# Mirrored filter rows fetched through copies in DRAM instead of reversed on TensorE, with three small edits at the kernel's opening

## The chip, the cores and the metric

The kernel runs on one core of one Trainium2 chip. The metric is the device time of one execution in microseconds (us). The kernel before takes 127.81 us, the median of 3 runs (127.77 to 128.35).

A core has five engines that run their own instruction lists in order and wait for one another through semaphores: TensorE (PE, with its weight loads listed as PEld), VectorE (DVE), ScalarE (ACT), GpSimd (POOL, unused here beyond four memsets) and SyncE (SP). SP only issues DMA transfers in this kernel. ACT issues a few of them at the start and the last one.

## The reference

```python
x = A_x                                             # [1, 2048, 512] bf16
g = sigmoid((x * gate_w).sum(-1, keepdims=True))
X = rfft2(x.astype(f32), axes=(-2, -1))             # [1, 2048, 257] complex
a = irfft2(X * (w_r + 1j * w_i), s=(2048, 512)).astype(bf16)
h = layernorm(x)                                    # over the 512 columns
u = gelu(einsum("bsd,sf->bdf", h, w1) + b1)         # f: 1792
b = (einsum("bdf,fs->bds", u, w2) + b2).transpose(0, 2, 1)
out = g * a + (1 - g) * b
```

Two branches share x. Branch a is a spectral filter: a two-dimensional real FFT over 2048 rows and 512 columns, a product with a complex filter W of 2048 rows and 257 columns, and the inverse FFT. Branch b is a token mixer: a layernorm, a matrix product that contracts the 2048 rows with `w1`, a GELU, and a product with `w2` back to 2048 rows. A gate per row mixes the two.

## The kernel before, in words

Row s of x is split as s = 512 q + 4 p + r: q from 0 to 3, r from 0 to 3, and p on the 128 partitions. A "row group" below is the 128 rows of one (q, r), 128 x 512 elements.

Branch b has two products. The first (function `m1`, line 705) accumulates over the 16 row groups for each of 14 blocks ft of 128 of the 1792 columns of `w1`. The second (`m2`, line 1011) accumulates over the 14 blocks for each of the 16 output row groups. Together they are the bulk of TensorE's work and need little from the other engines.

Branch a is a chain over the engines:

1. DVE combines the four q of x (lines 535 to 542), TensorE applies DFT tables along the rows (lines 554 to 557), ACT copies the result out of PSUM (line 560), and DVE combines again (line 566).
2. A radix-4 step on DVE for each of two frequency classes lt = 0 and 1 (function `radix4`: part e1 in lines 585 and 586, part e2 in lines 590 and 591, part e3 in lines 597 and 598).
3. A DFT along the columns on TensorE (line 653), once for each lt and each of four e. It reads what part e2 (for even e) or part e3 (for odd e) wrote. ACT copies it out (line 660), DVE combines it (lines 669 to 677).
4. The product with the filter on DVE (lines 820 to 842), then the inverse chain: radix-4 on DVE, line 890 to 898 on TensorE, 904 and 906 on ACT, and so on to line 1030.

The product with the filter works on a pair of mirrored frequencies at once, so each row of W is needed twice: at its own place and, for the mirrored frequency, in reversed order of the partitions. Tile `W` has for both parts of W (comp 0: real, comp 1: imaginary), for each lt and e, a slot 0 (own order) and a slot 1 (mirrored). In the kernel before the mirrored slot is filled in two ways. For lt = 1, four DMAs of 128 rows read the DRAM rows backwards. For lt = 0, the rows are loaded into a staging tile `wt` in natural order, TensorE multiplies them with a reversed identity matrix `flip` (functions `wf`, line 757, and `wfn`, line 767), and ACT copies the result from PSUM into `W` (lines 761 and 770). Function `ld_W` issues 16 DMAs for one comp, each of rows of 257 elements, that is 514 bytes.

`wprep` (lines 777 to 781) halves one row of `W` and forms sums and differences of the two slots at the columns 0 and 256 for two later tiny products. It needs all of `W`, for both comps and both slots.

The order of the work is not written by hand. Each piece is a task (`add`) with an engine, an assumed duration, the tasks that it depends on and a priority. A planner (`Plan.order`) runs a simple list schedule: at each moment it gives each free engine the ready task with the lowest priority number. The resulting order is emitted, and each engine then runs its list strictly in that order. For DMAs the planner assumes one rate for the bytes, one stream for all transfers, and that a DMA can be issued only when the eighth before it has landed. That last rule is real in the program: the transfers take turns on eight semaphores, and each waits, on the issuing engine, until the previous user of its semaphore has landed.

At the opening, `warm` (line 356) runs 10 matmuls over a tile of zeros, `presq` (line 361) takes the square root of a constant on ACT, so that the table of the square root is loaded early, and the row groups (q = 0, r = 0) and (q = 2, r = 0) come in two halves of 64 partitions each, one half on SP's queue and one on ACT's. The layernorm statistics of the first group start with line 487, the root is in line 511, the first normalised group in line 521.

Of the kernel before, what the change touches and what calls it, by code (L numbers as in the profile page):

```python
# [264 lines left out]
def kernel(  # L265
# [23 lines left out]
    pool = ctx.enter_context(tc.tile_pool(name="sb", bufs=1))  # L289
    psum = ctx.enter_context(tc.tile_pool(name="ps", bufs=1, space=bass.MemoryType.PSUM))  # L290
    NES = 2

    def sb(shape, dt, tag, bufs=1):
        return pool.tile(shape, dt, tag=tag, name=tag, bufs=bufs)
# [13 lines left out]
    def alloc_first():  # L308
# [19 lines left out]
        t["wt"] = sb([P, 2, 4, WL], BF16, "wt")  # L328
# [28 lines left out]
    NWARM = 10  # L357
    add("PE", 0.42 * NWARM, warm, reads=["warm", "xs"], writes=["warmed"], prio=-5, alloc=["fa"], free=["fa"])

    def presq():  # L360
        A.activation(t["ombb2"][:, 0:1], t["eps"][:], ActF.Sqrt, bias=t["eps"][:, 0:1], scale=1.0)
    add("ACT", 0.05, presq, reads=["eps"], writes=["omg"], prio=-5)


    Q0 = (0, 2, 1, 3)
    for q in (0, 2):
        for n in range(2):
            hp = slice(n * P // 2, (n + 1) * P // 2)
            ld([("xh", q, n)], lambda hp=hp, q=q: t["x"][hp, q, 0, :], x4[hp, q, 0, :], 65536, -9.5 + 0.1 * q, ("SP", "ACT")[n])
        add("DVE", 0.0, lambda: None, reads=[("xh", q, 0), ("xh", q, 1)], writes=[("x", 0, q)], prio=-9)  # L370
# [62 lines left out]
    def ld_W(comp):  # L433
        v = wsrc[comp].rearrange("(e c k) l -> c e k l", e=4, k=4)
        z = wsrc[comp].rearrange("(v u w) l -> w u v l", v=4, u=2)

        def emit():
            W, u = t["W"][:, comp], t["wt"][:, comp]
            dma(u[64:127, :, 0:257], v[65:128, :, 0, :])
            dma(u[0:64, :, 0:257], v[64:128, :, 2, :])  # L440
            dma(u[127:128, 0:2, 0:257], z[0:1, 1, 2:4, :])
            dma(u[127:128, 3:1:-1, 0:257], z[0:1, 0, 0:4:3, :])
            for e in range(4):
                dma(W[:, 1, e, 1, 0:257], v[:, 3 - e, 3, :].rearrange("(o i) l -> o i l", o=4)[:, ::-1])
            for o in range(4):
                dma(W[32 * o:32 * o + 32, 1, :, 0, 0:257], v[96 - 32 * o:128 - 32 * o, :, 1, :])
            dma(W[1:64, 0, :, 0, 0:257], v[1:64, :, 0, :])
            dma(W[64:128, 0, :, 0, 0:257], v[0:64, :, 2, :])
            dma(W[0:1, 0, :, 0, 0:257].rearrange("w (u v) l -> w u v l", u=2), z[0:1, :, 0:2, :])
            dma(t["wn"][:, comp, 0:257], wsrc[comp][1024:1025, :])  # L450
        return emit

    for comp in range(2):
        add("SP", 12.3, ld_W(comp), writes=[("W", comp), ("wt", comp)], prio=17 + 8 * comp, nbytes=300000, after=[a0])
        if comp == 0:
            load_wb(1)
# [292 lines left out]
    for comp in range(2):  # L749
        for lt in (0,):  # L750
            for a in range(2):
                tag = ("fa", "fb")[a]

                def wf(comp=comp, lt=lt, a=a, tag=tag):
                    pw = t["pw", comp, lt, a] = ps([P, 2, L], F32, tag, 2)
                    for i in range(2):
                        T.matmul(pw[:, i], lhsT=t["flip"][:], rhs=t["wt"][:, comp, 3 - 2 * a - i, 0:L], start=True, stop=True)
                add("PE", mm(256, 256), wf, reads=[("wt", comp), "flip"], writes=[("pw", comp, lt, a)], prio=5, alloc=[tag])

                def wfe(comp=comp, lt=lt, a=a):  # L760
                    A.copy(t["W"][:, comp, lt, 2 * a:2 * a + 2, 1, 0:L], t["pw", comp, lt, a][:])
                add("ACT", act(512), wfe, reads=[("pw", comp, lt, a)], writes=[("W~", comp, lt)], prio=3, free=[tag])

    def wfn():
        pw = t["pwn"] = ps([P, 4, 2], F32, "fa", 2)
        for e in range(4):
            T.matmul(pw[:, e], lhsT=t["flip"][:], rhs=t["wt"][:, :, 3 - e, 256], start=True, stop=True)
    add("PE", mm(*[4] * 4), wfn, reads=[("wt", 0), ("wt", 1), "flip"], writes=["pwn"], prio=5, alloc=["fa"])
    wtk = [("W~", comp, 0) for comp in range(2)]
    add("ACT", 0.3, lambda: A.copy(t["W"][:, :, 0, :, 1, 256], t["pwn"][:].rearrange("p e k -> p k e")),  # L770
        reads=["pwn"], writes=wtk, prio=3, free=["fa"])

# [9 lines left out]
    add("DVE", 0.8, wprep, reads=[], writes=[("W", 0), ("W", 1), "wpm"] + wtk, prio=1)  # L782


    for lt in range(2):
# [37 lines left out]
        for comp in range(2):  # L823
            def mul(lt=lt, comp=comp):
                xs = xph(0).rearrange("p (k c l) -> p k c l", k=8, c=2)
                o = (xph(1) if comp == 0 else t["st"][:]).rearrange("p (k c l) -> p k c l", k=8, c=2)
                w = t["W"][:, comp, lt].rearrange("p e s l -> p (e s) l")[:, :, None, 0:L].to_broadcast([P, 8, 2, L])
                V.tensor_mul(o, xs, w)
            add("DVE", tt(4096), mul, reads=["xs", ("W", comp), ("W~", comp, lt)], writes=[("pp", "st")[comp]], prio=pr)
# [249 lines left out]
```

## Time and profile before

| | before |
|---|---|
| median of 3 runs | 127.81 us (127.77 to 128.35) |
| the profiled execution's own time | 127.68 us |
| its span | 125.9 us |
| PE busy | 120.5 us (96%) |
| DVE busy | 113.8 us (90%) |
| ACT busy | 81.0 us (64%) |
| bytes by DMA | 23.12 MB, mean 184 GB/s |

The span runs from the first to the last instruction of the program; the 1.8 us between it and the execution's own time lie around it. Starts in the profile are counted from the span's start. "SPq" rows are the DMA-issuing instructions of SP: their length is the time that SP's sequencer spends on issuing, not the transfer. A PE row's length includes the pipeline's drain, so that two matmuls in a row overlap: the distance between their starts is the cost, 0.216 us for 512 columns.

### The profile page before, as it was taken

The numbers are of one execution on the slowest core, as the hardware profiler recorded it, in microseconds if no ns is written. First come the engines' busy times: TensorE is split into PE (matmuls) and PEld (weight loads), VectorE is DVE, ScalarE is ACT, GpSimd is POOL, SyncE is SP. The second block draws the span as 40 slices with busy tenths as digits, with TensorE's granted clock in tenths as the row PEclk, the third lists the DMA queues.
The fourth block names the chain that finished last, engine by engine and source line by source line (L and its number), as shares of the span: only waits on it lengthen the run. The fifth ranks groups of instructions, "written<-read, shape, count | busy, mean of one in ns | idle before, by whom it ended". The sixth has DMA issues, their size and how long they took to land.

```text
span 125.9 us, 2138 instructions
## 1 busy us (share of the span) xinstructions
PE 120.5 (96%) x743; PEld 68.8 (55%) x756; DVE 113.8 (90%) x273; ACT 81.0 (64%) x165; POOL 0.2 (0%) x4
## 2 busy tenths in 40 slices
PE   6899999999999999999999999999999999999991
PEld 2344555555655476644445555555577767655590
DVE  2699999999999999999999999999988999999651
ACT  0973689699999999999420004722299999952200
POOL 0000000000000000000000000000000000000000
PEclk9999999999999999999999999999999999999999
DMA  1999999994459946799999900000000000006541
GB/s 57 305 371 358 382 365 358 348 315 86 117 119 288 268 86 162 210 413 411 410 408 407 389 25 0 5 0 0 3 0 0 0 5 0 0 21 229 200 180 44
DMA packets 18219, 23.12 MB, mean 184 GB/s; under 512 B 2190, under 2 KB 15904, under 8 KB 18208
## 3 DMA queue, kind: packets, MB, share of 16 engines
q1 hardware_dynamic: 17616, 22.36, 52.6%
q10 hardware_dynamic: 592, 0.62, 1.6%
q8 instruction: 6, 0.10, 0.3%
q14 instruction: 5, 0.04, 0.1%
HBM read 20.86 MB, written 2.10 MB: 182 GB/s over the span
## 4 chain that ended last, share of the span: by engine, by line
PE 73%; DMA 17%; SPq 7%; issue 1%; DVE 0%
PE acc L1011 32%; PE acc L705 20%; DMA wa<-in_B_w_dram 9%; SPq L306 7%; PE fb L1011 5%; DMA wt<-in_A_w_r_dram 5%; DMA x<-in_A_x_dram 3%; PE fb L653 2%; PE fa L653 2%; PE fa L890 2%; PE fb L890 1%; PE fb L705 1%; PE fa L967 1%; PE fb L967 1%; PE fa L1011 1%
## 5 line engine op out<-in xcount | busy, mean ns | idle before, releaser
L705 PE MATMUL acc<-h,wb 128*128 128x512 bf16 x108 | 25.9, 379 | 0.1
L1011 PE MATMUL acc<-gl,wb 128*128 128x512 bf16 (+1 forms) x94 | 23.9, 371 | 0.2
L1011 PE MATMUL acc<-gl,wa 128*128 128x512 bf16 (+1 forms) x97 | 23.8, 371 | 0.1
L1017 ACT ACTIVATE x<-acc,ombb,omg 128x512 bf16<-128x512 f32 x12 | 9.1, 782 | 21.2 <-PE acc L1011 21.2
L1011 PEld LDWEIGHTS <-wa 128*128 128x128 bf16 x126 | 13.5, 113 | 9.9
L1011 PEld LDWEIGHTS <-wb 128*128 128x128 bf16 x126 | 13.3, 113 | 9.3
L705 PE MATMUL acc<-h,wa 128*128 128x512 bf16 x62 | 17.3, 379 | 0.1
L705 PEld LDWEIGHTS <-wb 128*128 128x128 bf16 x112 | 10.7, 98 | 10.6
L705 PEld LDWEIGHTS <-wa 128*128 128x128 bf16 x112 | 10.3, 98 | 10.7 <-DMA wa<-in_B_w_dram 0.8
L487 DVE BATCH_NORM_STATS2 stats<-x 128x6 f32<-128x512 bf16 x14 | 9.5, 679 | 2.1 <-DMA x<-in_A_x_dram 2.0
L560 ACT CAST xp<-fa 128x512 bf16<-128x512 f32 x16 | 9.1, 581 | 1.8 <-PE fa L557 1.8
L735 ACT ACTIVATE x<-x 128x512 bf16<-128x512 bf16 x16 | 10.2, 691 | 0.0
L721 ACT ACTIVATE gl<-acc,b1f 128x512 bf16<-128x512 f32 x11 | 7.9, 718 | 3.2 <-PE acc L705 3.2
L705 PE MATMUL fb<-h,wa 128*128 128x512 bf16 x31 | 9.5, 379 | 0.1
L527 ACT ACTIVATE h<-x,nmr,rstd 128x512 bf16<-128x512 bf16 x11 | 8.4, 808 | 1.1 <-DMA wb<-in_B_w_dram 0.8
L705 PE MATMUL fa<-h,wa 128*128 128x512 bf16 x16 | 5.9, 378 | 0.7 <-DVE h L521 0.6
L653 PEld LDWEIGHTS <-X 128*128 128x128 bf16 x64 | 4.7, 98 | 2.1
L974 ACT ACTIVATE B<-fb,g 128x512 bf16<-128x512 f32 x8 | 5.7, 713 | 0.0
L974 ACT ACTIVATE B<-fa,g 128x512 bf16<-128x512 f32 x8 | 5.6, 705 | 0.1
L660 ACT CAST X<-fb 128x512 bf16<-128x512 f32 x8 | 5.1, 634 | 0.0
L660 ACT CAST X<-fa 128x512 bf16<-128x512 f32 x8 | 5.0, 620 | 0.0
L356 PE MATMUL fa<-xp 128*128 128x512 bf16 x10 | 3.8, 549 | 1.2 <-DVE xp L317 1.2
(169 smaller groups left out, 232.7 us busy)
## 6 DMA issues: line engine op xcount, KB each, us to landing
wb<-in_B_w_dram SPq DMA_DIRECT2D x11, 512.0 KB
wa<-in_B_w_dram SPq DMA_DIRECT2D x7, 512.0 KB
wa<-in_B_w_dram SPq DMA_DIRECT2D x2, 896.0 KB
wb<-in_B_w_dram SPq DMA_DIRECT2D x4, 384.0 KB
out_dram<-x SPq DMA_DIRECT2D x3, 512.0 KB
x<-in_A_x_dram SPq DMA_DIRECT2D x2, 512.0 KB
wa<-in_B_w_dram SPq DMA_DIRECT2D x2, 448.0 KB
rot<-dft_ti SPq DMA_DIRECT2D x1, 768.0 KB
```

What stands on the lines that cost most here:

```text
L306: (eng or nc.sync).dma_start(out=out_ap, in_=in_ap)
L487: V.bn_stats(out=t["stats"][:, j, :], in_=t["x"][:, j // 4, j % 4, :])
L527: add("ACT", 0.71, lambda j=j: A.activation(t["h"][:, j // 4, j % 4, :], t["x"][:, j // 4, j % 4, :], ActF.Identity, bias=t["nmr"][:, j:j ...
L560: add("ACT", act(512), lambda r=r, dq=dq: A.copy(xe(r)[:, :, :, dq, :], t["pa", r, dq][:]), reads=[("pa", r, dq)], writes=[("X", r, dq)], ...
L653: T.matmul(pb[:, k % 2, k // 2], lhsT=t["X"][:, lt, EX[e], c, k, :], rhs=tbl(k, c), start=True, stop=True)
L660: A.copy(t["X"][:, lt, EX[e]].rearrange("p c j l -> p (c j l)").rearrange("p (h c g b) -> p h c g b", h=2, c=2, b=2)[:, :, c], t["pb", lt, ...
L705: T.matmul(t["u", ft][:], lhsT=w[:, j // 4, j % 4, c * P:(c + 1) * P], rhs=t["h"][:, j // 4, j % 4, :], start=(j == jorder[0]), stop=(j == ...
L721: gelus.append(add("ACT", act(512, 1) , lambda ft=ft: A.activation(t["gl"][:, ft, :], t["u", ft][:], ActF.Gelu_apprx_tanh, bias=t["b1f"][: ...
L735: A.activation(t["x"][:, q, r, :], t["x"][:, q, r, :], ActF.Copy, accum_out=t["glog"][:, 4 * q + r:4 * q + r + 1])
L974: A.activation(eo_v(p)[:, n], t["i3", j][:], ActF.Copy, scale=t["g"][:, j:j + 1])
L1011: T.matmul(t["y", j, m][:, cs], lhsT=w[:, o, 512 * q + r:512 * q + 512:4], rhs=t["gl"][:, ft, cs], start=(ft == 0), stop=(ft == NFT - 1))
L1017: A.activation(tbuf(j).rearrange("p h d -> p (h d)"), t["y", j, 0][:], ActF.Identity, bias=t["ombb2"][:, j:j + 1], scale=t["omg"][:, j:j + 1])
```

## The change

- The mirrored slot of both lt is loaded, and nothing is reversed on TensorE. `wf`, `wfn`, their copies on ACT and the staging tile `wt` go.
- For each comp two new DRAM scratch tensors: `fe` (4 x 128 rows) and `fo` (16 x 32 rows). `ld_flip` issues, for each comp, two DMAs from DRAM to DRAM that write rows of W in reversed order into `fe` (the rows for lt = 0) and `fo` (those for lt = 1).
- `ld_nat` issues the loads in natural order, 10 DMAs for each comp, among them the two single-row pieces of the mirrored slot.
- `ld_mir` issues three loads for each comp from `fo` and `fe` into the mirrored slots.
- In the emitted order of SP the four copies come first, where the first load of `wt` was, then the natural loads of comp 0, the four loads of `wb` (the last three blocks of `w1`), the natural loads of comp 1, and the six mirrored loads. The loads of the tables `ti` and `tg` now stand ahead of four loads of `w2`.
- The two first row groups come as one DMA each, q = 0 on SP's queue and q = 2 on ACT's.
- `presq` goes, and `NWARM` is 9 instead of 10.
- All orders follow from the planner. On DVE, `wprep` moves: it stood behind the last combination of line 677, and now stands in the radix-4 step of lt = 1 between part e1 (lines 585 and 586) and part e2 (lines 590 and 591). On TensorE five more matmuls of line 705 come before the first of line 653 for lt = 1: 53 instead of 48 counted from the first that reads `wb`.

```diff
-        t["wt"] = sb([P, 2, 4, WL], BF16, "wt")
...
-    NWARM = 10
+    NWARM = 9
...
-    def presq():
-        A.activation(t["ombb2"][:, 0:1], t["eps"][:], ActF.Sqrt, bias=t["eps"][:, 0:1], scale=1.0)
-    add("ACT", 0.05, presq, reads=["eps"], writes=["omg"], prio=-5)
...
     for q in (0, 2):
-        for n in range(2):
-            hp = slice(n * P // 2, (n + 1) * P // 2)
-            ld([("xh", q, n)], lambda hp=hp, q=q: t["x"][hp, q, 0, :], x4[hp, q, 0, :], 65536, -9.5 + 0.1 * q, ("SP", "ACT")[n])
-        add("DVE", 0.0, lambda: None, reads=[("xh", q, 0), ("xh", q, 1)], writes=[("x", 0, q)], prio=-9)
+        ld([("x", 0, q)], lambda q=q: t["x"][:, q, 0, :], x4[:, q, 0, :], 131072, -9.5 + 0.1 * q, "ACT" if q else "SP")
...
-    def ld_W(comp):
+    def ld_flip(comp):
+        ev = wsrc[comp].rearrange("(e m w) l -> w e m l", e=4, w=2)[0, :, P:2 * P, :]
+        od = wsrc[comp].rearrange("(g i k) l -> k g i l", i=32, k=4)[3]
+
+        def emit():
+            fe = t["fe", comp] = dram.tile([4, P, 257], BF16, tag=f"fe{comp}", name=f"fe{comp}")
+            fo = t["fo", comp] = dram.tile([16, 32, 257], BF16, tag=f"fo{comp}", name=f"fo{comp}")
+            dma(fe[:], ev[:, ::-1])
+            dma(fo[:], od[:, ::-1])
+        return emit
+
+    def ld_nat(comp):
...
-            dma(u[64:127, :, 0:257], v[65:128, :, 0, :])
-            dma(u[0:64, :, 0:257], v[64:128, :, 2, :])
-            dma(u[127:128, 0:2, 0:257], z[0:1, 1, 2:4, :])
-            dma(u[127:128, 3:1:-1, 0:257], z[0:1, 0, 0:4:3, :])
-            for e in range(4):
-                dma(W[:, 1, e, 1, 0:257], v[:, 3 - e, 3, :].rearrange("(o i) l -> o i l", o=4)[:, ::-1])
...
+            dma(W[0:1, 0, 0:2, 1, 0:257], z[0:1, 0, 0:4:3, :])
+            dma(W[0:1, 0, 3:1:-1, 1, 0:257], z[0:1, 1, 2:4, :])
...
+    def ld_mir(comp):
+        def emit():
+            W, fe, fo = t["W"][:, comp], t["fe", comp], t["fo", comp]
+            m = fe[:].rearrange("e (p two) l -> two p e l", two=2)
+            dma(W[:, 1, ::-1, 1, 0:257], fo[:].rearrange("(e o) i l -> (o i) e l", e=4))
+            dma(W[1:64, 0, ::-1, 1, 0:257], m[1, 0:63])
+            dma(W[64:128, 0, ::-1, 1, 0:257], m[0, 0:64])
+        return emit
+
+    FL = (16, 16.1)
     for comp in range(2):
-        add("SP", 12.3, ld_W(comp), writes=[("W", comp), ("wt", comp)], prio=17 + 8 * comp, nbytes=300000, after=[a0])
+        add("SP", 1.1, ld_flip(comp), writes=[("flp", comp)], prio=FL[comp], nbytes=700000, after=[a0])
+    for comp in range(2):
+        add("SP", 5.5, ld_nat(comp), writes=[("W", comp)], prio=17 + 8 * comp, nbytes=300000, after=[a0])
+        add("SP", 1.6, ld_mir(comp), reads=[("flp", comp)], writes=[("W~", comp)], prio=26 + comp, nbytes=500000)
         if comp == 0:
             load_wb(1)
...
-    add("DVE", 0.8, wprep, reads=[], writes=[("W", 0), ("W", 1), "wpm"] + wtk, prio=1)
+    add("DVE", 0.8, wprep, reads=[], writes=[("W", 0), ("W", 1), ("W~", 0), ("W~", 1), "wpm"], prio=1)
```

The functions `wf` and `wfn` with their tasks are deleted from the program.

## The prediction

> **What bounds the kernel now.** I read the page's busy shares first, then the chain, then the waits, and then the timelines of SP, DVE and PE around the place where the filter is loaded.
>
> ```profile
> span 125.9 us, 2138 instructions
> PE 120.5 (96%) x743; PEld 68.8 (55%) x756; DVE 113.8 (90%) x273; ACT 81.0 (64%) x165; POOL 0.2 (0%) x4
> ...
> PE 73%; DMA 17%; SPq 7%; issue 1%; DVE 0%
> ```
>
> PE has work for 96% of the span, and the chain lies on it for 73%; its links through DMA and SP are from the loading phase. PE never waits long after the opening, so it is the bound: matmuls taken away are worth their full length, and every us in which PE has to wait later is added in full. DVE is close behind, in a chain that PE reads from.
>
> The loading of the filter, on SP:
>
> ```profile
> 24.90 2.56 SPq L306 DMA_DIRECT2D wt<-in_A_w_r_dram  x4
> 27.95 7.55 SPq L306 DMA_DIRECT2D W<-in_A_w_r_dram  x11
> 35.55 0.42 SPq L306 DMA_DIRECT2D wn<-in_A_w_r_dram  x1
> 36.01 2.62 SPq L306 DMA_DIRECT2D wb<-in_B_w_dram  x4
> 38.68 2.54 SPq L306 DMA_DIRECT2D wt<-in_A_w_i_dram  x4
> 41.27 8.55 SPq L306 DMA_DIRECT2D W<-in_A_w_i_dram  x11
> 49.87 0.42 SPq L306 DMA_DIRECT2D wn<-in_A_w_i_dram  x1
> ```
>
> (Columns: start, length, instruction.) SP issues without rest from 24.9 to 50.3 us: one DMA takes it 0.35 to 0.69 us. And it waits: of its waits between 24 and 51 us the first is
>
> ```profile
> SPq L306 <- DMA wb<-in_B_w_dram: 4.4, 4, 1.5
> ```
>
> 4.4 us in 4 waits, each for the eighth DMA before. So a slow transfer holds up everything that SP issues from the eighth place behind it.
>
> DVE, where `wprep` stood and where it will stand:
>
> ```profile
> 44.82 1.22 DVE L586 TENSOR_TENSOR st<-X 128x2048 bf16<-128x2048 bf16 x1
> 46.07 0.69 DVE L590 TENSOR_TENSOR X<-xp 128x1024 bf16<-128x1024 bf16 x1
> 46.68 0.68 DVE L591 TENSOR_TENSOR X<-xp 128x1024 bf16<-128x1024 bf16 x1
> ...
> 57.46 0.41 DVE L777 TENSOR_SCALAR W<-W 1x1028 bf16<-1x1028 bf16 x1
> 57.91 0.19 DVE L780 TENSOR_TENSOR wpm<-W 128x16 f32<-128x16 bf16 x1
> 58.21 0.19 DVE L781 TENSOR_TENSOR wpm<-W 128x16 f32<-128x16 bf16 x1
> ```
>
> At 57.5 us all of `W` has been there for long and `wprep` waits for nothing. Its new place is between lines 586 and 590, at 46.1 us.
>
> **The change part by part.**
>
> *Matmuls removed.* Eight of line 757 and four of line 767:
>
> ```profile
> 53.02 0.38 PE L757 MATMUL fa<-wt,flip 128*128 128x256 bf16 x2
> 53.24 0.38 PE L757 MATMUL fb<-wt,flip 128*128 128x256 bf16 x2
> 53.46 0.38 PE L705 MATMUL acc<-h,wb 128*128 128x512 bf16 x1
> 53.67 0.24 PE L767 MATMUL fa<-wt,flip 128*128 128x2 bf16 x4
> 53.78 0.81 PE L705 MATMUL acc<-h,wb 128*128 128x512 bf16 x3
> ```
>
> By the starts, two of line 757 cost 0.22 us and the four of line 767 some 0.2 us at most: 8 x 0.108 + 0.2 = 1.07 us off PE. The five copies on ACT also go; ACT is 64% busy, so that is worth nothing by itself.
>
> *The opening.* The first real matmul (5.56 us) waits for the first normalised group, which hangs on x's first group (statistics start at 3.48) and on ACT's root at 4.58. The halves landed at 2.95 and 3.35 us by their semaphores; one whole load has twice the rows on one queue and shares the transfer engines with the other group: 0 to 0.5 us later. Against it, `presq` (0.30 us at 4.38) no longer stands before the root, and the table load, which waits for nothing, starts earlier, since ACT issues one DMA fewer (0.6 us). The tenth matmul over zeros ended at 4.98, before 5.56, so it was hidden. Between -0.3 and +0.5; I take 0.
>
> *SP's new order and the wait that `wprep` gets.* This decides. `wprep` now needs the last of the six mirrored loads. I follow SP from 24.90, where the first copy is issued.
>
> (a) Which transfer engines carry the copies? The nearest rows are the four 128-row loads from 27.95 on: their DRAM side has an outer dimension of 4, as the `fe` copies have, and each raised its semaphore once early and then four times (30.94, 30.96, 31.48, 31.50 for the first), so four engines carried it, 32 rows each. The last rises of the next three are at 32.77, 34.15 and 35.25: 1.2 us for 32 rows, 37 ns a row; the packets of 514 bytes themselves took 28 ns in the median. I take 34 ns. An `fe` copy then puts 128 rows on each of these four engines, and an `fo` copy (outer dimension 16) 32 rows on every engine: 2 x (128 + 32) = 320 rows in line on four engines, 10.9 us. They start when `b2h`, ahead of them, is through (rises from 28.15 on, take 28.7): the last copy lands at 39.6.
>
> The Trainium skill (DMA: Bandwidth & Descriptors, "Why a DMA increments its semaphore by 16 and not by 1", on how many engines) says that a DMA is spread over the largest number up to 16 that divides the outer dimension of both sides. It would put `fe` on 4 engines and `fo` on 16. The four rises agree; no row of this trace is a copy from DRAM to DRAM.
>
> (b) The first single-row piece of comp 0 is eight places behind the last copy, so it goes at 39.6. With two more issues (0.63, 0.63, 0.42 and 0.05 between) 41.4; the four of `wb` take 2.62, the last starts at 43.4 and SP is free at 44.1.
>
> (c) The same piece of comp 1 is eight behind the last `wb`. That one was issued at 38.01 before and landed between 43.7 (14 engines) and 45.56 (the last two), 5.7 to 7.5 us: here 49.1 to 50.9, take 50.0. The seven issues between need only 3.7 us.
>
> (d) Three issues (1.83) to 51.8, then the six mirrored loads: by the forms of 512, 252 and 256 rows 0.63, 0.54 and 0.63, so the last starts at 55.0. A load of that form was issued at 48.48 and landed at 51.67: 3.2 us. The mirror is complete at 58.2.
>
> (e) DVE stands at `wprep` from 46.1 to 58.2, then does line 781 (0.2) and lines 590 and 591 (1.29 from 46.07 to their end): 59.8. On PE the matmuls of line 653 for lt = 1 wait for that. PE gets there at: 35.63 (first with `wb`) + 42 x 0.216 + 16 x 0.055 + 0.65 + (16 x 0.055 + 3 x 0.216) + 5 x 0.216 = 48.85. Behind it in PE's list stand all 51 matmuls of line 705 that are left and the whole second product: they could run, and cannot pass. PE waits 59.9 - 48.85 = 11.05 us.
>
> What would cover this? ACT and DVE do nothing that PE could use; PE's fillers are behind the waiting instruction. The loads of `w2` start some 5 us later (55.7 instead of 50.4), but their reader (64.5) is moved by 11 us, so they stay hidden.
>
> *After the wait.* Does PE come back at full pace? The opening shows it from rest: weight loads at 1.62, 2.04, 2.47, 2.90, 3.32, 3.75 and 4.18, so 0.43 us for a 512-column matmul, against 0.216 later. After the pause of 0.57 us before 5.56 the pace was 0.216. So between 0 and 7 x 0.21 = 1.5 us; a pause of 11 us is nearer the first, I take 1.5.
>
> The Trainium skill (TensorE: Matmul & The Clock Gate, "Part 1: The HAM clock gate") says that PE falls to half its clock after an idle window of about 3.4 us and needs about as long at work to come back. By it the sum is the one below; without a fall it would be 137.7. The opening agrees; no long pause within the kernel is in this trace.
>
> *Sum,* against the profiled execution's 127.68 (0.13 below the median of the runs): 127.68 - 1.07 + 0 + 11.05 + 1.5 = 139.2 us.
>
> **Rivals.**
>
> 1. *The copies are spread over 16 engines.* Then 128 rows stand on each, they are done by 33.1 and hold up nothing; `wb` starts at 35.3, the single-row piece of comp 1 goes at 43.9 behind the last `wb`, the last mirror is issued at 48.9 and lands at 52.1. PE waits 5.0 us: 131.6, and 130.6 if the last `wb` lands with the early engines. For it: `fe`'s DRAM target is one run of 512 rows. Against: the four rises above.
>
> 2. *Writing rows to DRAM is dearer.* A tenth of the 514-byte packets took 53 ns and more; at 53 ns the 320 rows take 17.0 us, 6.1 more: 145.3. For it: the trace has no such write; against: the packets of stores are not slower than those of loads.
>
> 3. *The mirror is there in time.* It decides in (e): with the last mirror landed by 47.3 us PE does not wait, and the time is 126.6; at 48.4 the matmuls saved are used up; every us later is a us more. If SP never had to wait, its issues would run 24.9 + 4 x 0.67 + 5.6 + 2.7 + 5.6 + 3.2 = 44.7 to the last and land at 47.9: 127.3, no change; with transfers that land a little faster, faster. For it: the issues alone nearly fit. Against: SP waited 4.4 us here already, for `wb` alone, and now has more bytes ahead.
>
> **How the numbers follow.** The forecast (last mirror at 56 to 60 us): 0.65. Rival 1: 0.13. Rival 2: 0.12. Rival 3: 0.10, half of it faster, half the same. About 0.5% (0.6 us) can be told from no change. Faster 0.05, same 0.05, slower 0.90. The range takes in rival 1 and most of rival 2: 130.5 to 145; the forecast's own is 136.5 to 141.5.
>
> **What would show it.** DVE: one idle time of some 12 us before line 781 (or 780), ended by a DMA into `W`. PE: an idle time of some 11 us before line 653, near 49 us, ended by DVE; then weight loads 0.43 us apart for some 3 us. SP: a gap of some 3.5 us that ends near 38.5 us, when the second `fe` copy lands, before the natural load of single rows that stands eight places behind it. No line 757 or 767 on PE. The forecast is wrong if DVE passes `wprep` without idle time, or if the copies raise their semaphores 16 times each within 2 us.

## The result, and the profile after

The changed kernel takes 143.29 us, the median of 6 runs (142.63 to 144.81); the kernel before took 127.79 us beside it (127.68 to 128.35). The ratio is 1.121, with a 95% interval of 1.115 to 1.127. The prediction was 139.2 us, with a range from 130.5 to 145. The profiled execution took 142.63 us. In the experiments below some profiled executions are longer than others of the same kernel; the ratios leave the longer ones out, and where a row is read from such an execution its time stands beside it.

Lines of the changed kernel are 12 higher than before up to the removed functions and 12 lower behind them: line 653 is now 665, 705 is 717, 590 is 602, 777 to 781 are 765 to 769, and 1011 is 999.

From the page of the changed kernel: the span, the busy times, and the chain by engine.

```profile
span 140.8 us, 2108 instructions
PE 122.7 (87%) x743; PEld 68.9 (49%) x743; DVE 113.5 (81%) x273; ACT 79.5 (56%) x159; POOL 0.2 (0%) x4
...
PE 53%; DMA 27%; SPq 15%; issue 1%; DVE 1%; ACTq 1%; DVEq 0%
```

PE was at work for 96% of the span and is at 87%. The chain now lies on DMA and SP for 42% where it was 24%: in the middle of the kernel, PE follows the loads.

SP's timeline of the changed kernel over the filter's loads (start, length, instruction):

```profile
24.50 0.75 SPq L307 DMA_DIRECT2D fe<-in_A_w_r_dram  x1
25.30 3.76 SPq L307 DMA_DIRECT2D fo<-in_A_w_r_dram  x1
29.10 0.85 SPq L307 DMA_DIRECT2D fe<-in_A_w_i_dram  x1
30.00 4.32 SPq L307 DMA_DIRECT2D fo<-in_A_w_i_dram  x1
34.36 7.48 SPq L307 DMA_DIRECT2D W<-in_A_w_r_dram  x9
...
42.34 2.62 SPq L307 DMA_DIRECT2D wb<-in_B_w_dram  x4
45.00 6.80 SPq L307 DMA_DIRECT2D W<-in_A_w_i_dram  x9
...
52.30 0.66 SPq L307 DMA_DIRECT2D W<-fo  x1
...
55.27 1.42 SPq L307 DMA_DIRECT2D W<-fe  x2
56.79 4.32 SPq L307 DMA_DIRECT2D wa<-in_B_w_dram  x7
```

The first natural load is issued at 34.36. In the kernel before, SP's first load of the filter went at 24.90 and its last at 49.87. Two single instructions, the issues of `fo`, hold SP for 3.76 and 4.32 us. Behind them SP waits another 1.7 us, until 39.81, for the landing of the second `fe` copy, whose semaphore the seventh natural load takes.

DVE's timeline of the changed kernel at `wprep`; the brackets give the idle time ahead and what ended it:

```profile
44.95 1.22 DVE L598 TENSOR_TENSOR st<-X 128x2048 bf16<-128x2048 bf16 x1
53.41 0.42 DVE L765 TENSOR_SCALAR W<-W 1x1028 bf16<-1x1028 bf16 x1 [7.24 <-DMA W<-in_A_w_i_dram]
58.69 0.18 DVE L768 TENSOR_TENSOR wpm<-W 128x16 f32<-128x16 bf16 x1 [4.86 <-DMA W<-fo]
61.77 0.19 DVE L769 TENSOR_TENSOR wpm<-W 128x16 f32<-128x16 bf16 x1 [2.90 <-DMA wa<-in_B_w_dram]
61.87 0.69 DVE L602 TENSOR_TENSOR X<-xp 128x1024 bf16<-128x1024 bf16 x1
```

`wprep` waits three times, 15.0 us together: for the natural loads of comp 1, the mirror of comp 0 and the mirror of comp 1. (The last wait is put down to a load of `w2` that landed at about the same moment; the last semaphore rise of the sixth mirrored load is at 61.65.) Line 602, which PE needs, follows.

PE's timeline at the same place:

```profile
47.68 1.24 PE L717 MATMUL acc<-h,wb 128*128 128x512 bf16 x5
62.62 0.61 PE L665 MATMUL fa<-tb,X 128*128 128x128 bf16 x4 [13.70 <-DVE X L602]
63.02 0.63 PE L717 MATMUL acc<-h,wb 128*128 128x512 bf16 x1
63.44 0.63 PE L665 MATMUL fb<-tb,X 128*128 128x128 bf16 x4
...
67.26 0.39 PE L665 MATMUL fa<-tb,X 128*128 128x128 bf16 x4
```

PE stands for 13.70 us, and afterwards a matmul of 512 columns costs 0.43 us (63.02 to 63.44) where it cost 0.216. That lasts 4.64 us for work that takes 2.62 us at the usual pace. The sum closes: 127.68 - 1.07 + 13.70 + 2.0 = 142.3, against 142.63.

### The profile page after: what moved, and what is told of

It reads as the page before. It is cut to its first block, busy times and chain, and to the rows that moved or that the text cites. A ratio compares the mean times of both kernels' runs of the same rounds, so it can differ in the third digit from the quotient of the medians.

```text
span 140.8 us, 2108 instructions
## 1 busy us (share of the span) xinstructions
PE 122.7 (87%) x743; PEld 68.9 (49%) x743; DVE 113.5 (81%) x273; ACT 79.5 (56%) x159; POOL 0.2 (0%) x4
## 4 chain that ended last, share of the span: by engine, by line
PE 53%; DMA 27%; SPq 15%; issue 1%; DVE 1%; ACTq 1%; DVEq 0%
PE acc L999 29%; SPq L307 15%; DMA wa<-in_B_w_dram 11%; PE acc L717 10%; DMA fe<-in_A_w_i_dram 8%; PE fb L999 5%; DMA wb<-in_B_w_dram 4%; DMA W<-fe 4%; PE fa L878 1%; PE fb L878 1%; PE fa L665 1%; PE fb L665 1%; PE fb L955 1%; PE fa L955 1%; ACTq L307 1%
## 5 line engine op out<-in xcount | busy, mean ns | idle before, releaser
L717 PE MATMUL acc<-h,wb 128*128 128x512 bf16 x112 | 27.3, 392 | 0.0
L1005 ACT ACTIVATE x<-acc,ombb,omg 128x512 bf16<-128x512 f32 x12 | 9.7, 824 | 19.9 <-PE acc L999 19.9
L665 PE MATMUL fa<-tb,X 128*128 128x128 bf16 x32 | 3.6, 242 | 13.7 <-DVE X L602 13.7
L717 PE MATMUL fb<-h,wa 128*128 128x512 bf16 x32 | 10.0, 379 | 0.0
L962 ACT ACTIVATE B<-fb,g 128x512 bf16<-128x512 f32 x8 | 7.0, 874 | 0.0
L962 ACT ACTIVATE B<-fa,g 128x512 bf16<-128x512 f32 x8 | 7.0, 870 | 0.0
```

The lines of the kernel that those rows point to most:

```text
L665: T.matmul(pb[:, k % 2, k // 2], lhsT=t["X"][:, lt, EX[e], c, k, :], rhs=tbl(k, c), start=True, stop=True)
L717: T.matmul(t["u", ft][:], lhsT=w[:, j // 4, j % 4, c * P:(c + 1) * P], rhs=t["h"][:, j // 4, j % 4, :], start=(j == jorder[0]), stop=(j == ...
L962: A.activation(eo_v(p)[:, n], t["i3", j][:], ActF.Copy, scale=t["g"][:, j:j + 1])
L1005: A.activation(tbuf(j).rearrange("p h d -> p (h d)"), t["y", j, 0][:], ActF.Identity, bias=t["ombb2"][:, j:j + 1], scale=t["omg"][:, j:j + 1])
```

## The experiments

The first four share 17 runs of the kernel before (127.87 us), the next four share 7 (127.69), the last four share 13 (127.81).

### The opening alone

The kernel before with the three small edits only:

```diff
-        for n in range(2):
-            hp = slice(n * P // 2, (n + 1) * P // 2)
-            ld([("xh", q, n)], lambda hp=hp, q=q: t["x"][hp, q, 0, :], x4[hp, q, 0, :], 65536, -9.5 + 0.1 * q, ("SP", "ACT")[n])
-        add("DVE", 0.0, lambda: None, reads=[("xh", q, 0), ("xh", q, 1)], writes=[("x", 0, q)], prio=-9)
+        ld([("x", 0, q)], lambda q=q: t["x"][:, q, 0, :], x4[:, q, 0, :], 131072, -9.5 + 0.1 * q, "ACT" if q else "SP")
...
-    add("ACT", 0.05, presq, reads=["eps"], writes=["omg"], prio=-5)
...
-    NWARM = 10
+    NWARM = 9
```

> The kernel before with the three edits at the opening alone (whole loads of the two row groups on two queues, no early root, nine zero products). Theory: they are worth next to nothing, the first real matmul starts 0.1 us earlier as in the changed kernel (5.45 against 5.56 us): 127.6 us, between 127.3 and 128.0. Rival: part of the 15 us comes from the opening, by a later first group or a different order: over 129 us.

Measured: 127.75 us (127.43 to 129.24, 12 runs), ratio 0.9999 with the interval 0.9975 to 1.0023. The opening is worth nothing, as the prediction took it. All of the change in time belongs to the filter's rows.

### `wprep` behind the last combination again

The changed kernel with `wprep` pinned where it stood before:

```diff
-    add("DVE", 0.8, wprep, reads=[], writes=[("W", 0), ("W", 1), ("W~", 0), ("W~", 1), "wpm"], prio=1)
+    add("DVE", 0.8, wprep, reads=[], writes=[("W", 0), ("W", 1), ("W~", 0), ("W~", 1), "wpm"], prio=1, after=[pl.last_w["B", 1, 3]])
```

> The changed kernel with the copies as they are, but wprep ordered behind the last combination on DVE, where it stood before. Theory: the cost is the wait of wprep at its early place; the mirror still lands near 61.7 us, DVE gets to wprep near 57.7 us and waits some 4 us, of which PE, which reads DVE's results next near 88 us, pays about 3: 130 us, between 128.5 and 131.5, and no slow matmuls near 62 us. Rival: the copies cost by themselves (their traffic delays other loads): 138 us or more.

Measured: 145.16 us (143.66 to 145.83), ratio 1.131 with the interval 1.125 to 1.136. The expectation fell: the wait of 13.7 us is gone from line 665, and the time is no shorter. The groups of waits of this kernel (the profiled execution took 145.83) show where it went; the columns are the us waited in total, how often, and the longest:

```profile
...
PEld L999 <- DMA wa<-in_B_w_dram: 9.5, 7, 2.0
PE acc L999 <- DMA wa<-in_B_w_dram: 6.5, 7, 1.5
...
DVE wpm L768 <- DMA W<-fo: 5.2, 1, 5.2
```

PE comes to the second product in time and finds no `w2`. On SP the seven loads of `w2` into `wa` were issued at 62.21 (before: 50.40), behind the copies, the natural loads and the mirror. PE takes each as it lands:

```profile
59.67 6.21 PE L717 MATMUL acc<-h,wb 128*128 128x512 bf16 x28
67.35 0.41 PE L999 MATMUL acc<-gl,wa 128*128 128x512 bf16 x1 [1.48 <-DMA wa<-in_B_w_dram]
68.62 0.41 PE L999 MATMUL acc<-gl,wa 128*128 128x512 bf16 x1 [0.86 <-DMA wa<-in_B_w_dram]
69.90 0.61 PE L999 MATMUL acc<-gl,wa 128*128 128x512 bf16 x1 [0.87 <-DMA wa<-in_B_w_dram]
```

One matmul for every 1.27 us, the time in which 512 KB land. So the place of `wprep` decides only which reader of SP's late loads waits. The prediction took the `w2` loads as hidden because "their reader (64.5) is moved by 11 us"; this run is the case in which the reader is not moved by a wait.

### `fe` on sixteen engines

The changed kernel, with the `fe` copies written with an outer dimension of 16 like `fo` (as many rows of the same size, but other rows than the mirrored table needs):

```diff
-            dma(fe[:], ev[:, ::-1])
+            dma(fe[:].rearrange("e (o i) l -> (e o) i l", o=4), wsrc[comp].rearrange("(g i k) l -> k g i l", i=32, k=4)[0][:, ::-1])
```

> The changed kernel with the two fe copies reading as many rows with an outer dimension of 16 instead of 4, so that 16 engines carry them. It copies other rows into the scratch, so the mirrored filter of lt = 0 is not the reference's; amounts and order of all work are the same. Theory: SP was held up by copies on four engines; now they end near 34 us, SP issues the last mirrored load near 49 to 50 us instead of 56.1, it lands near 54.5 instead of 61.7, and PE's wait shrinks from 13.7 to about 7: 136 us, between 134 and 138. Rival: rows written to DRAM are dear on whatever engine: 141 us or more.

Measured: 143.8 us (141.65 to 144.38), ratio 1.114 with the interval 1.107 to 1.121. The expectation fell. SP's timeline of this kernel:

```profile
28.09 1.20 SPq L307 DMA_DIRECT2D fo<-in_A_w_i_dram  x1
29.33 11.91 SPq L307 DMA_DIRECT2D W<-in_A_w_r_dram  x9
41.30 0.41 SPq L307 DMA_DIRECT2D wn<-in_A_w_r_dram  x1
```

The copies are issued without the long holds (1.20 us for the last), but the natural loads take 11.91 us instead, and SP is done with them at nearly the same moment, 41.71 against 42.30. By their semaphores the four copies land at 39.98; in the changed kernel they land at 40.43. The engines that carry `fe` raise its semaphore 16 times here; in the changed kernel it rose once early and four times late (32.16 to 33.78 for comp 0). So `fe` was on four engines, as the prediction's step (a) had it, and it made no difference: 2048 rows of 514 bytes, from DRAM to DRAM, are through at 40 us with 320 of them in line on four engines or with 128 in line on each of sixteen. The stretch from 29 to 34 us shows how, first in the changed kernel, then in this one. The columns are the length, the busy time of PE, PEld, DVE, ACT and POOL, PE's clock, the DMA share and GB/s:

```profile
29.00:34.00 5.00, 5.00 (x37) 3.01 (x36) 5.00 (x9) 4.99 (x9) 0.00 (x0) 1.00 0.47 102
29.00:34.00 5.00, 5.00 (x36) 2.99 (x34) 5.00 (x9) 4.82 (x10) 0.00 (x0) 1.00 1.24 112
```

The DMA share is the packets' time as a share of sixteen engines' time. It is 0.47 where four engines have a long line and the others a short one, and 1.24 here. But the rows move hardly faster: a packet of 514 bytes took 62 ns here in the median of that stretch, where it took 28 ns in the changed kernel. So more engines shortened the line and lengthened the row. What slows the rows on sixteen engines is not shown by any run.

### The copies from GpSimd's queue

The copies are issued by GpSimd from 22.9 us on, and `wprep` is pinned late as in the second experiment:

```diff
-            dma(fe[:], ev[:, ::-1])
-            dma(fo[:], od[:, ::-1])
+            if comp == 0:
+                t["pw"] = sb([1, 8], BF16, "pw")
+                nc.gpsimd.tensor_copy(t["pw"][:], t["gw"][0:1, 0:8])
+            dma(fe[:], ev[:, ::-1], nc.gpsimd)
+            dma(fo[:], od[:, ::-1], nc.gpsimd)
...
-        add("SP", 1.1, ld_flip(comp), writes=[("flp", comp)], ...)
+        add("POOL", 1.1, ld_flip(comp), reads=["gw"], writes=[("flp", comp)], ...)
...
+    add("DVE", 0.8, wprep, ..., prio=1, after=[pl.last_w["B", 1, 3]])
```

> The changed kernel with the four copies issued from GpSimd's queue behind a tiny copy of a piece of gw (landed near 21 us), and wprep at its late place. Theory: SP is not held up, the mirror is complete by about 50 us, wprep waits for nothing at 57.5 us, and the removed matmuls are what is left: 126.6 us, between 126.2 and 127.2, faster than the kernel before. Rival: the copies' share of the four engines delays the last blocks of w1 or the loads of w2 and PE waits elsewhere: 128.5 us or more.

Measured: 144.08 us (141.13 to 145.38), ratio 1.122 with the interval 1.116 to 1.128. The expectation fell again. SP's timeline (the profiled execution took 141.13):

```profile
24.36 17.14 SPq L307 DMA_DIRECT2D W<-in_A_w_r_dram  x9
...
56.69 3.65 SPq L307 DMA_DIRECT2D wa<-in_B_w_dram  x6
```

SP is no longer held by the copies' issue, and its first nine natural loads take 17 us all the same: one of them, of 256 rows, holds it for 4.13 us at its issue, and it waits 5.3 us for `b2h`, the load ahead of them, which was issued at 23.89 and landed at 40.23. The first natural load was issued at 24.36 and landed at 40.86. Another queue does not take the copies off the path of SP's loads. The Trainium skill (DMA: Bandwidth & Descriptors, "Queues, rings and completion order") says that each transfer engine takes turns, packet by packet, between the queues that have work for it; the trace agrees, in which packets of both queues start in every microsecond from 27 to 39 us, while that load needs 16.5 us. `w2` follows at 56.69, 6 us late, and PE waits for it as in the second experiment.

### Without the copies

The copies are left out, the mirrored loads stay where they are and read the weights as they lie:

```diff
-            fe = t["fe", comp] = dram.tile(...)
-            fo = t["fo", comp] = dram.tile(...)
-            dma(fe[:], ev[:, ::-1])
-            dma(fo[:], od[:, ::-1])
+            t["fe", comp], t["fo", comp] = ev, od
```

> The four DRAM copies are left out; the six mirrored loads keep their place and their sizes and read rows of the weights as they lie, so the mirrored half of the filter table holds the wrong rows. Order on PE, DVE and ACT as in the changed kernel. Theory (the copies' own time on the DMA path is what comes late): SP starts on the natural loads at 24.5 in place of 34.36, all behind them is 9.9 us earlier, PE's wait in front of line 665 falls from 13.7 to about 3.8 and the clock stays up: 142.6 - 9.9 - 2.0 = 130.7, between 129 and 133. Rival (the mirrored loads in their new place behind w1's last blocks are late by themselves): the wait stays over 10 us and the time over 138.

Measured: ratio 1.0425 with the interval 1.035 to 1.050, that is 5.4 us over the kernel before. The four executions lie apart, at 132.93, 133.84, 137.34 and 138.29; the ratio is that of the first two, and the profiled one is that of 137.34. By the ratio the copies are worth 10.1 of the 15.5 us (1.121 against 1.0425); by the other two executions it would be 5 to 6 us. The theory was right in sign, but 5.4 us are left that it did not foresee in full. In the profiled execution PE's wait has shrunk but not gone:

```profile
PE fa L662 <- DVE X L599: 7.4, 1, 7.4
DVE wpm L765 <- DMA W<-in_A_w_r_dram: 5.5, 1, 5.5
DVE wpm L766 <- DMA wa<-in_B_w_dram: 3.4, 1, 3.4
```

`wprep` still waits 8.9 us for the mirrored loads, which are issued from 45.36 to 49.84 behind 20 natural loads and four of `wb`, and land until 55.1. So the new order on SP has a price of its own, even with no copies.

### Without the copies, `wprep` late

The edits of the second and the fifth experiment together:

```diff
-            dma(fe[:], ev[:, ::-1])
-            dma(fo[:], od[:, ::-1])
+            t["fe", comp], t["fo", comp] = ev, od
...
+    add("DVE", 0.8, wprep, ..., prio=1, after=[pl.last_w["B", 1, 3]])
```

> As the run without copies, and the line of wprep pinned behind the last step of the first product's DVE work, as in the second experiment (wrong mirrored rows again). Theory: nothing is late any more, w2's loads are issued at about 46 (before: 50.40), and what is left is the saving of the nine matmuls: 126.6, between 126 and 127.8. Rival (the pinned place costs by itself, by which the second experiment could be explained): w2 in time and still over 133.

Measured: 134.26 us (133.65 to 135.74), ratio 1.048 with the interval 1.042 to 1.053. The theory's 126.6 fell, and so did its rival as it was put: `w2` is not in time. Its `wa` loads are issued at 50.53, as before, but the first lands at 56.95 in place of 54.09, since the mirrored loads ahead land until 55.97. And SP's timeline goes on (the profiled execution took 135.74):

```profile
50.53 4.82 SPq L307 DMA_DIRECT2D wa<-in_B_w_dram  x7
55.99 0.33 SPq L307 DMA_DIRECT2D rot<-dft_ti  x1
56.97 0.32 SPq L307 DMA_DIRECT2D tg<-dft_tg  x1
58.30 9.06 SPq L307 DMA_DIRECT2D wb<-in_B_w_dram  x7
```

In the kernel before the first loads into `wb` were issued at 54.19, ahead of `ti` and `tg`. PE stands for them at the second product (4.7 us in three waits, the longest 3.2). Apart from the later landing, two differences could be behind this: that order on SP, or PE's own order, which takes the blocks of `w2` one after the other here. The runs with `w2` first and with `ti` first, below, bear on them.

### Half the copies, `wprep` late

Only `fe` stays; the mirrored rows of lt = 1 are loaded directly, as in the kernel before:

```diff
-            dma(fo[:], od[:, ::-1])
...
+            for e in range(4):
+                dma(W[:, 1, e, 1, 0:257], v[:, 3 - e, 3, :].rearrange("(o i) l -> o i l", o=4)[:, ::-1])
...
-            dma(W[:, 1, ::-1, 1, 0:257], fo[:].rearrange("(e o) i l -> (o i) e l", e=4))
```

> Only the copies fe stay; the reversed half of odd rows is loaded straight from the weights with the four loads for each component that the kernel before has; wprep pinned late. Theory (dose): half the copied rows, so half of their 15.9 us; w2's loads are issued at about 50 to 54 in place of 62.2, up to 4 us later than before: 127 to 133. Rival (a fixed price as soon as anything is copied through DRAM, by waiting for its completion): as the second experiment, over 140.

Measured: 142.48 us (141.32 to 143.31), ratio 1.112 with the interval 1.103 to 1.120. Half the copied rows saved little, against the theory's dose. By the semaphores the two `fe` copies land at 38.29, only 2.1 us earlier than all four: 256 rows stand in line on four engines, where there were 320. That is 33 ns for each of the 64 rows fewer, and the DMA share from 31 to 35 us is 0.26, about four engines of sixteen: here the line on four engines binds. Then 28 natural loads instead of 20 have to go, and `w2` is issued at 60.17. A copy of half the rows on the same four engines gains little.

### The copies into SBUF

As the run without copies, but 2048 rows are loaded into a scrap tile in SBUF at the copies' place:

```diff
+            if comp == 0:
+                t["se"] = sb([P, 2, 4, 257], BF16, "se")
+            dma(t["se"][:, 0], ev.rearrange("e m l -> m e l"))
+            dma(t["se"][:, 1], od.rearrange("(e o) i l -> (o i) e l", e=4))
```

> The same 2048 rows of 514 bytes are copied at the same place of SP's queue, but into a scrap tile in SBUF and not reversed; the mirrored loads read the weights as they lie, as in the run without copies (wrong mirrored rows). Theory (writing rows to DRAM is what is dear): 128 rows on each of 16 engines at the 34 ns of the loads of before = 4.4 us in place of 15.9; SP's natural loads start about 28 to 30, PE's wait is 6 to 8 us: 133 to 137. Rival (a row costs the same wherever it goes, the number of rows is what counts): as the changed kernel, 141 to 144.

Measured: ratio 1.084 with the interval 1.075 to 1.093, or 10.7 us over the kernel before. That lies about midway between the run without copies (5.4) and the changed kernel (15.5), between theory and rival. But it is not the price of the rows alone. The scrap tile is one for both components, so the loads of comp 1 wait until those of comp 0 have landed, a wait that the copies into DRAM do not have. SP's waits from 24 to 40 us (the profiled execution took 152.51):

```profile
SPq L307 <- DMA se<-in_A_w_r_dram: 4.4, 2, 4.1
```

What can be compared is the first half. By the semaphores the 1024 rows of comp 0 land at 31.62 in SBUF, and at 35.91 in DRAM (the run with `fe` on sixteen engines), both issued between 23.7 and 25.5 us behind the same loads. This speaks for rows into DRAM being slower; how much of the copies' cost that makes was not measured.

### Without the copies, `wprep` late, `w2` ahead of `ti` and `tg`

The kernel of the sixth experiment, with the loads of `ti` and `tg` bound to the end of the matmuls that free the first buffer of `wb`:

```diff
-    load("tg", [P, 642], BF16, tabs["tg"], 164352, prio=39.5)
...
-    add("SP", 0.2, ld_ti, writes=["ti"], prio=39, nbytes=754176, after=[...])
+    m4 = [m1t[order.index((NF + 3, jorder[-1]))]]
+    add("SP", 0.2, ld_ti, writes=["ti"], prio=39, nbytes=754176, after=m4 + [...])
+    load("tg", [P, 642], BF16, tabs["tg"], 164352, prio=39.5).deps.update(m4)
```

> As the sixth experiment (no copies, wrong mirrored rows, wprep pinned late), and the loads of ti and tg put back behind the four loads of w2 that the kernel before issues ahead of them. Theory (what was left there is the second product starving for w2: its loads into wb were issued at 58.30 behind ti and tg, in the kernel before at 54.19 ahead of them): the wb loads are issued at about 55.4, PE waits at most 2 us for them, and the time is 126.6 to 129. Rival (the wait comes from the amount of data ahead of the second product, whatever the order, as the whole of w2 starts at 50.5 in both): 132 or more.

Measured: 131.30, 133.65, 133.92 and 133.94 us. The order on SP is that of the kernel before (the `wb` loads are issued at 53.93), and the time is still 3.5 to 6 us over it: 131.30 lies between theory and rival, the other three in the rival's range. PE's timeline of the execution of 133.94:

```profile
63.34 1.67 PE L997 MATMUL acc<-gl,wa 128*128 128x512 bf16 x7
65.54 0.41 PE L997 MATMUL acc<-gl,wb 128*128 128x512 bf16 x1 [0.53 <-DMA wb<-in_B_w_dram]
66.83 0.41 PE L997 MATMUL acc<-gl,wb 128*128 128x512 bf16 x1 [0.88 <-DMA wb<-in_B_w_dram]
68.10 0.49 PE L997 MATMUL acc<-gl,wb 128*128 128x512 bf16 x1 [0.87 <-DMA wb<-in_B_w_dram]
69.36 0.62 PE L997 MATMUL acc<-gl,wb 128*128 128x512 bf16 x1 [0.77 <-DMA wb<-in_B_w_dram]
69.78 3.19 PE L997 MATMUL acc<-gl,wa 128*128 128x512 bf16 x7
```

PE reads seven blocks of `wa` and then, one by one, four of `wb`. The kernel before does the same work in another order (its PE timeline):

```profile
64.35 2.11 PE L1011 MATMUL acc<-gl,wa 128*128 128x512 bf16 x9
66.30 0.38 PE L1011 MATMUL acc<-gl,wb 128*128 128x512 bf16 x1
66.51 1.24 PE L1011 MATMUL acc<-gl,wa 128*128 128x512 bf16 x5
67.59 0.81 PE L1011 MATMUL acc<-gl,wb 128*128 128x512 bf16 x3
```

It already works on the next row groups with the blocks that are there, needs `wb` later and at a slower rate, and never waits. So PE's order of the second product is another thing that moved with the plan.

### The kernel before with `ti` and `tg` first

```diff
-    load("tg", [P, 642], BF16, tabs["tg"], 164352, prio=39.5)
+    load("tg", [P, 642], BF16, tabs["tg"], 164352, prio=34.3)
...
-    add("SP", 0.2, ld_ti, writes=["ti"], prio=39, ...)
+    add("SP", 0.2, ld_ti, writes=["ti"], prio=34.2, ...)
```

> The kernel before with one thing changed: ti and tg are loaded ahead of all seven wb loads of w2, as in the changed kernel. Theory: the four wb loads are issued at about 57 to 58 in place of 54.19 and land some 3 us later; the second product, which reads the first of them at 66.30, waits for them some 2 to 4 us: 129 to 132. Rival (before has slack enough): 127.8, no change.

Measured: 127.71 us (127.69 to 128.32, 10 runs), ratio 0.9986 with the interval 0.9964 to 1.0007. The rival's number held: `ti` and `tg` ahead of `w2`'s `wb` loads cost nothing, although the first of those loads went out at 55.95 and landed at 67.20, later than in the run before this one (65.49). But the planner moved PE's order along with the edit:

```profile
64.37 4.48 PE L1011 MATMUL acc<-gl,wa 128*128 128x512 bf16 x20
68.69 0.59 PE L1011 MATMUL acc<-gl,wb 128*128 128x512 bf16 x2
```

PE runs twenty matmuls on `wa` before it asks for `wb` at 68.69; the kernel before asks at 66.30, after nine. So late `wb` loads cost nothing where PE asks for them late, and earlier ones were waited for in the run with `w2` first. This points to PE's order of the blocks; no run changed that order alone.

### Work for PE during the wait

Fifty-six matmuls on a table that lies there are put in front of the first matmul of line 665 for lt = 1; their result is not used:

```diff
                     pb = t["pb", lt, e, c] = ps([P, 2, 2, 2, 64], F32, tag, 2)
+                    if (lt, e, c) == (1, 0, 0):
+                        for _ in range(56):
+                            T.matmul(pb[:].rearrange("p a b c d -> p (a b c d)"), lhsT=t["tb"][:, 0:P], rhs=t["tb"][:, 0:512], start=True, stop=True)
```

> The changed kernel with 56 matmuls on data that lie there (result not used), put in front of the first matmul of line 665 for lt=1, so that PE works through most of its wait of 13.7 us. If the slow matmuls after that wait (0.43 us each in place of 0.216 for about 4.6 us) come from the pause, they are gone and the time falls by 2.0 us to about 140.6. Rival: the slow matmuls come from something else at that place, or the clock is taken back elsewhere: no change, 142.6 to 143.3.

Measured: 145.58 us (144.93 to 147.6), ratio 1.134 with the interval 1.128 to 1.141. Inconclusive on the price: the mirror landed 2.2 us later in the profiled execution (line 602 at 64.11 against 61.87), so PE still stood for 4.09 us behind the extra matmuls. A table by stretches of this kernel, with the columns of the table above:

```profile
48.50:60.70 12.20, 12.20 (x57) 5.36 (x55) 0.42 (x1) 1.05 (x3) 0.00 (x0) 1.00 0.69 150
60.70:64.80 4.10, 0.06 (x1) 0.00 (x0) 0.98 (x4) 0.00 (x0) 0.00 (x0) 0.78 1.04 295
64.80:70.00 5.20, 5.15 (x27) 3.01 (x28) 5.20 (x16) 2.77 (x6) 0.00 (x0) 0.52 1.03 409
```

The clock was full to the end of the extra work, and a pause of 4.1 us brought it to 0.52 for the next 5 us, with matmuls 0.43 us apart. The slow stretch thus follows a pause of 4.1 us as it does one of 13.7. Nor is it the place: in the second experiment line 665 for lt = 1 has no wait ahead, and from 48.07 us on its groups of four cost 0.22 us each. The Trainium skill (TensorE: Matmul & The Clock Gate, "Part 1: The HAM clock gate") gives an idle window of about 3.4 us for the fall; the pause of 4.1 us agrees. That its price is 2.0 us rests on the pace in the changed kernel alone, since no run took it away. Why the mirror came later was not settled; SP's natural loads of comp 1 took 9.11 us here and 6.80 in the profile of the changed kernel, and they took between 6.8 and 10.0 us in other kernels too.

### The copies in long rows

The same 1.05 MB from DRAM to DRAM, in 64 rows of 16,448 bytes:

```diff
-            dma(fe[:], ev[:, ::-1])
-            dma(fo[:], od[:, ::-1])
+            src = wsrc[comp][0:512, :].rearrange("(g i) l -> g (i l)", g=16)
+            src2 = wsrc[comp][512:1024, :].rearrange("(g i) l -> g (i l)", g=16)
+            dma(fe[:].rearrange("e (o i) l -> (e o) (i l)", o=4), src)
+            dma(fo[:].rearrange("g i l -> g (i l)"), src2)
```

> The four copies move the same 1.05 MB from DRAM to DRAM at the same place, in rows of 16,448 bytes in place of 514, not reversed; the mirrored loads read them as before (wrong mirrored rows). Theory (a copy is dear by the row): 64 rows in place of 2048, the copies take 3 to 5 us in place of 15.9, and the time comes near that of the run without copies: 133 to 136. Rival (dear by the byte written to DRAM): 141 to 144.

Measured: 133.69, 138.34, 138.47 and 138.81 us. The lowest and the highest lie 0.8 and 0.5 us over those of the run without copies (132.93 and 138.29), and all lie some 4.5 us or more under the changed kernel's median. Only 133.69 is in the theory's range; the other three lie between theory and rival. In the profiled execution (138.81) the four copies are issued in 0.59 to 1.03 us each, the first natural load goes at 28.14 in place of 34.36, and the copies land at 32.61 in place of 40.43. So a copy through DRAM is not dear by the byte, as the theory said. That the row's length is what counts is not quite separated: the edit also takes away the reversed order of the rows and the stride between them. The exact size is open too, since the four executions lie 5 us apart.

None of these versions beats the kernel before. Its saving would be the 1.07 us of the matmuls, and even without copies the loads cost more than that.

## Why the prediction was right, and where it was off

The mechanism came as predicted: PE waits once, for DVE at `wprep`, for the last mirrored load. The size came less well: 143.29 lies in the stated range, which was wide because it took in two rivals, and outside the forecast's own 136.5 to 141.5. Point by point:

- *Matmuls removed, -1.07*, and *the opening, 0*. The sum closes with the first; the opening alone measured 0.9999.
- *(a) Copies.* `fe` on four engines: shown by its four late rises. The last copy was forecast to land at 39.6 and landed at 40.43. The row's price came out at 37 to 50 ns for the 320 rows in line, depending on whether they started at 28.7 (where step (a) put it) or at their issue (24.5). The run with half the copies agrees: 64 rows fewer in line, 2.1 us earlier. What does not follow is that more engines would help: on sixteen the copies land at the same time, with slower rows.
- *(b), (c).* SP was to be free at 44.1 behind `wb` and was at 44.96. The single-row piece of comp 1 was to go at 50.0, and went at 50.56, when the last `wb` had landed. The wait that was named as a sign came too, for the second `fe` copy, but took 1.7 us and ended at 39.81 where 3.5 us and 38.5 were forecast. One thing was missing: SP was first held for 8.1 us inside the two issues of `fo`. It was the landing that let SP go on, so these holds changed the delay little; in the run with `fe` on sixteen engines they are gone, and SP is through the natural loads at nearly the same moment.
- *(d) The last mirrored load.* It was issued at 56.10 (forecast 55.0) and landed at 61.65 (58.2). Its landing time is the term that was mis-sized: 3.2 us was that of a single load, and measured were 5.6. The six mirrored loads bring 2040 rows behind one another, and the last stands at the end of that line: they landed at 55.54, 57.44, 58.47, 59.80, 60.77 and 61.65.
- *(e) PE's wait.* PE came to line 665 at 48.92 (forecast 48.85) and waited 13.70 (11.05): the late landing less the 0.7 us that DVE and PE were quicker from the landing to the first matmul. Step (e) let PE wait for both lines of part e2; the first matmul came at 62.62, with line 602 done and line 603 still running. And DVE's wait came in three pieces, where one of some 12 us was named as the sign.
- *After the wait, 1.5.* Measured 2.0: the right mechanism, the slow stretch is longer than the one at the opening.
- Together: 2.65 + 0.5 of the 3.4 us by which 139.2 fell short of the profiled 142.63; the remaining 0.3 is not placed. The landing times that the prediction reads for the two halves of x, 2.95 and 3.35, are one semaphore rise short of the last (2.99 and 3.38), which changes no term.

Of the rivals, the first (copies spread, 131.6) was run as an experiment: even with sixteen engines the copies hold up as much. Its sum also left out the slow stretch after a pause of 5 us, for which a pause of 4.1 us was enough in the run with work for PE. The second (writes dearer) may have part of the truth, since 1024 rows landed 4.3 us later in DRAM than in SBUF; but in the changed kernel the copies landed only 0.8 us later than the forecast. The third needed the mirror by 47.3 us, and even without copies it lands at 55.1 us.

What the prediction did not see is that the wait at `wprep` hid two others. It wrote that the `w2` loads "stay hidden" because their reader is moved by 11 us, which was right for this kernel; but whoever takes the wait away meets late `w2` loads (second and fourth experiment) and a second product whose order on PE no longer seems to spare them (the run with `w2` first).

## What to carry to other kernels

When a load that many others queue behind becomes slow, moving the instruction that waits for it does not help: the next reader behind the same queue waits as long (13.7 us at line 665 gone, and 143.29 us became 145.16). Before trading matmuls for a reversal through DRAM, count its rows: 2048 rows of 514 bytes cost 10 us here by the ratios, against 1.07 us of TensorE, and neither more engines nor another queue changed that, while long rows in natural order did. When a planner sets the order, compare the lists of all engines far behind the edit too; here the order of the second product had changed without a line of it being edited.

## What the runs showed of the hardware that was not expected

- SP can be held inside a single DMA issue, with no semaphore to wait for: 3.76 and 4.32 us for `fo`, 4.23 us for the second of two `fe` copies, 0.59 us for as many bytes in long rows, and 4.13 us for a plain load of 256 rows beside copies on another queue.
- More engines need not move rows faster: 2048 rows of 514 bytes from DRAM to DRAM land at 40.43 us with the half of them on four engines and at 39.98 with all on sixteen, both begun at about 24 us. From 29 to 34 us a packet of 514 bytes took 28 ns in the first and 62 ns in the second (medians).
- PE's clock can fall without one long pause: in the run with `w2` first no wait in the stretch is over 0.88 us, but there is one matmul for each 1.27 us, and the next seven take 3.19 us in place of 1.67, with a granted clock of 0.50 from 69.7 to 73.0 us. In the run with half the copies no wait of PE from 62 to 74 us is over 1.48 us, and the clock is 0.50 from 70 to 74.
